# Ranks of a gate line by two comparisons a tile, from a line that each partition reads one element further on

## The chip, the cores and the metric

The kernel runs on one core of one Trainium2 chip. The metric is device time in microseconds (us) of one execution; several runs are made and the median is given. The engines of a core are TensorE (PE; PEld is its weight load), VectorE (DVE), ScalarE (ACT), GpSimd (POOL) and SyncE (SP), which issues most DMAs. Each engine works through its own instructions in program order and waits for others by semaphores.

## The reference

Attention with queries pooled in pairs, and behind it a mixture-of-depths layer: in each batch the 128 tokens with the highest gate scores go through a two-layer network, and the others pass unchanged.

```python
B, H, S, D = 8, 8, 1152, 64                       # attention
q_pool = q.reshape(B, H, S // 2, 2, D).mean(axis=3)
scores = q_pool @ k.T / sqrt(D)
attn = softmax(scores)                            # over the keys
x = (attn @ v), heads side by side                # (8, 576, 512)

scores = einsum('bsd,d->bs', x, w_gate)           # mixture of depths, F = 1024, capacity = 128
for b in range(B):
    top_idx = argpartition(-scores[b], capacity)[:capacity]
    xe = x[b, top_idx]
    ye = maximum(xe @ w1, 0) @ w2
    g = 1 / (1 + exp(-scores[b, top_idx]))
    out[b, top_idx] = x[b, top_idx] + g[:, None] * ye
```

## The kernel before

**Halves.** The work of the attention is cut into 8 batches x 4 pairs of heads x 2 halves of the 576 pooled queries: 64 halves, numbered from 0, eight to a batch. A method `run` writes out the order by hand; for half h it issues:

- at odd halves the loads of the pair after the next (`load_pair`: keys L744, queries L750, values L759) and the stores of an earlier pair (`stored`, L1023), all on SP;
- `scores`: 72 matmuls (L871) and nine exponentials on ScalarE (L878); they need the pair's `kT` and `qT`;
- `units("mid")`: pieces of the routing of earlier batches;
- `gated` (half h - 3) and `folded`: the sums of the exponentials. GpSimd adds two thirds of them in three instructions (`acc`, L910), VectorE sums the last third and then `acc` (`fold`, L915);
- at even halves `prepare_pair`: GpSimd pools the queries (L769), VectorE transposes keys into `kT` (L772) and queries into `qT` (L776);
- `weighted` (half h - 1): 72 matmuls with the values (L889); ScalarE copies the result (L897), GpSimd adds its two parts (L899), and `drained` transposes it on VectorE (L968);
- `normalized` and `divided` (L1012): the division by the sums, the latter on GpSimd;
- `units("end")`: more pieces of the routing.

**Routing.** `routed(b, part)` is a Python generator of one batch's routing. Each `yield` ends a piece; its value says where the next piece is issued: "mid", "sums" (between `folded` and `weighted`), or, for True, "end". One batch's pieces are thus spread over the halves of the next batch. The pieces are: the gate line of 576 scores is summed (L1067, L946) and written to HBM as a `row`; it is read back in two layouts, once whole into each partition (`sc_row`, L1083), and once token by token across partitions (`gate_sc`, L1084 and L1085: partition p has tokens p, 128 + p, and so on). The gate is max(score, -88) (L1099), an exponential (L1146), plus one (L1149) and a reciprocal. A token's rank is the number of tokens that come before it. For each of five tiles of 128 tokens (the last has 64), VectorE counts the tokens in earlier tiles with a score no lower (L1113), those from its own tile on with a higher score (L1122), and, by a triangular mask `before`, those of equal score earlier in its own tile (L1132, `tie`). Each count is two entries of the trace, the comparison and the read of its accumulator. Batches 0 to 5 cut this after tiles 1 and 3, batch 6 after tile 2, with `yield mid`, where `mid` is True for batches 6 and 7.

Ranks and gates go to HBM (L1162, `row_rank`) and come back in every partition (`lines`, L1166, 640 KB); two searches on VectorE (L1197) find the token and the gate of each slot; GpSimd gathers the tokens' rows by an indirect DMA (L1224); a copy through HBM and a transpose (L1237, L1254, L1262) turn them. In batch 7 the slots are found by a comparison `pick` (L1174) and matmuls with it (L1183) instead, with index and gate copied by ScalarE (L1190, L1191).

**The network.** Two batches are worked on together (`layers_of_two`, batches 0 and 1, and 2 and 3) by seven block products a layer (`seven_products`, L1358), with the weights' sums `tw` loaded in turn (L715). The result is added to the tokens' rows by `scaled` (L1451) and written back by an indirect DMA of GpSimd (`written`, L1300). Batches 4 and 5, and 6 and 7, are worked on in `ending`, where `first_layer` and `second_layer` (L1437, L1447) are generators too, and `pieces(unit, n)` issues n pieces of one. There `layer` is the first layer of batches 4 and 5, `third` that of 6 and 7, `second` a second layer, `old` what is left of batch 6's routing and `new` batch 7's. c11, c12, c21 and c22 are the quarters of a layer's result, s1 to s4 the sums that the next layer needs (`four_sums`, L1524). Values of the attention are stored (`stored`) before rows are gathered from the output.

Of the kernel before, what the change touches and what calls it, by code (L numbers as in the profile page):

```python
# [10 lines left out]
P = 128  # L11
BLK = 32

G = 3
F32 = mybir.dt.float32
# [6 lines left out]
def _rows_of(ap_1d: bass.AP, parts: int) -> bass.AP:  # L22

    return dataclasses.replace(ap_1d, ap=[[0, parts]] + [list(x) for x in ap_1d.ap])

# [509 lines left out]
class _Plain:  # L535
# [85 lines left out]
    def constants(self):  # L621
        nc, const = self.nc, self.const

        self.before = const.tile([P, P], F32, name="before")
        nc.gpsimd.memset(self.before[:, :], 1.0)
        nc.gpsimd.affine_select(
            out=self.before[:, :],
            in_=self.before[:, :],
            compare_op=ALU.is_gt,
            fill=0.0,  # L630
            base=0,
            pattern=[[-1, P]],
            channel_multiplier=1,
        )
# [39 lines left out]
    def weight_loads(self):  # L674
# [5 lines left out]
        for c in range(self.ND):  # L680
            yield self.nc.sync.dma_start(self.w1[:, c, :], w1[:, c, :])

# [326 lines left out]
    def divided(self, pair):  # L1009

        x = pair["x"] = self.work.tile([P, self.QB, BLK], F32, name="x")
        self.nc.gpsimd.tensor_tensor(  # L1012
# [44 lines left out]
    def routed(self, b, part):  # L1057
# [12 lines left out]
        sc = ffn.tile([P, NT], F32, name="gate_sc")  # L1070
# [6 lines left out]
        sc_row = ffn.tile([P, NT * P], F32, name="sc_row", bufs=1)  # L1077
        row = self.dram.tile([Sp], F32, name="row")
        nc.gpsimd.memset(sc[:, NF:], 0.0)
        nc.sync.dma_start(row.rearrange("(i n) -> i n", i=BLK), total[:, :])  # L1080

        def reads():
            nc.sync.dma_start(sc_row[:, 0:Sp], _rows_of(row[:], P))  # L1083
            nc.sync.dma_start(sc[:, 0:NF], row[0 : NF * P].rearrange("(t p) -> p t", p=P))  # L1084
            nc.sync.dma_start(  # L1085
                sc[0 : self.TAIL, NF:], row[NF * P :].rearrange("(t p) -> p t", p=self.TAIL)
            )
# [6 lines left out]
        if b < self.B - 2:  # L1094
# [5 lines left out]
            out=gate[:, :], in0=sc[:, :], scalar1=-88.0, scalar2=None, op0=ALU.max  # L1100
        )

        parts = ffn.tile([P, NT, 3], F32, name="rank_parts")
# [3 lines left out]
        rank = ffn.tile([P, NT], F32, name="rank")  # L1107
        for t, rows in tiles:
            at = t * P
            cmp = ffn.tile([P, Sp], F32, name="pick", bufs=1)  # L1110
            own = sc[0:rows, t : t + 1]
            if t > 0:
                nc.vector.tensor_scalar(  # L1113
                    out=cmp[0:rows, 0:at],
                    in0=sc_row[0:rows, 0:at],
                    scalar1=own,
                    scalar2=None,
                    op0=ALU.is_ge,
                    op1=ALU.add,
                    accum_out=parts[0:rows, t, 0:1],  # L1120
                )
            nc.vector.tensor_scalar(  # L1122
                out=cmp[0:rows, at:Sp],
                in0=sc_row[0:rows, at:Sp],
                scalar1=own,
                scalar2=None,
                op0=ALU.is_gt,
                op1=ALU.add,
                accum_out=parts[0:rows, t, 1:2],
            )  # L1130
            tie = ffn.tile([P, P], F32, name="pick", bufs=1)
            nc.vector.scalar_tensor_tensor(  # L1132
                out=tie[0:rows, 0:rows],
                in0=sc_row[0:rows, at : at + rows],
                scalar=own,
                in1=self.before[0:rows, 0:rows],
                op0=ALU.is_equal,
                op1=ALU.mult,
                accum_out=parts[0:rows, t, 2:3],
            )  # L1140
            cuts = (2,) if b == self.B - 2 else (1, 3)
            if t == cuts[0] < cuts[-1]:
                yield True
            if t == cuts[-1]:
                yield mid
# [687 lines left out]
```

## Time and profile before

| | |
|---|---|
| median of 3 runs | 689.88 us (689.51 to 690.7) |
| the profiled execution: time, span | 688.71 us, 686.9 us |
| mean granted TensorE clock | 0.994 of full speed |
| TensorE busy | 674.0 us (98%) |
| VectorE, GpSimd, ScalarE busy | 591.3 (86%), 501.1 (73%), 454.7 us (66%) |
| DMA, mean | 148 GB/s |

All times are from the start of the span, in us, durations in us unless marked ns. A line of the timeline has the start, the duration, engine, line of the kernel, operation, output <- input and shape, and in brackets the idle time of that engine before it, with what ended it. A line of groups ends with busy time in us, the mean of one in ns, and idle time before. A line of windows has the stretch, its length, busy time and count of PE, PEld, DVE, ACT and POOL, the granted TensorE clock, the mean number or share of the DMA queues at work, and GB/s. A value in the last columns is an average over the window.

Half h has its scores at about 7 us + 8.7 h, plus what the layers of batches 0 to 3 take in between; the scores of half 60 start at 585.14, those of half 63, the last, at 611.37, and `ending`'s first product stands at 624.57.

### The profile page before, as it was taken

How to read it: one execution, taken by the hardware profiler on the slowest of the kernel's cores; microseconds unless marked ns; L12 is line 12 of the kernel's file. 1: busy time of each engine (PE TensorE's matmuls, PEld its weight loads, DVE VectorE, ACT ScalarE, POOL GpSimd, SP SyncE). 2: the span in 40 equal slices, each digit the busy share in tenths (PEclk: the TensorE clock that was granted, in tenths of full speed). 3: DMA queues.
4: the chain of work that ended last, by engine and by line, in shares of the span. 5: the costliest groups of instructions: out<-in, count | busy, mean ns of one | idle time of the engine just before them, and what ended most of it. 6: DMA issues, size and time to landing. Idle time of an engine off the chain costs nothing.

```text
span 686.9 us, 23530 instructions
## 1 busy us (share of the span) xinstructions
PE 674.0 (98%) x9953; PEld 461.5 (67%) x9953; DVE 591.3 (86%) x880; ACT 454.7 (66%) x989; POOL 501.1 (73%) x485
## 2 busy tenths in 40 slices
PE   8999999999999999999999999999989999999996
PEld 6666666666666568676667768667657776668895
DVE  3878998999999986778899996696999999798864
ACT  5677777777777784837777776673767777873220
POOL 4788888879887883857798787393888879876011
PEclk9999999999999999999999999999999999999999
DMA  8888888858985885644988697571888848635210
GB/s 164 171 185 179 221 176 179 156 108 194 206 179 105 187 161 104 176 87 104 258 154 159 127 176 152 122 174 37 186 225 154 154 102 176 168 86 134 42 47 36
DMA packets 396642, 101.50 MB, mean 148 GB/s; under 512 B 376432, under 2 KB 380400, under 8 KB 395504
## 3 DMA queue, kind: packets, MB, share of 16 engines
q1 hardware_dynamic: 395008, 95.43, 67.0%
q0 software_dynamic: 1280, 4.20, 1.7%
q8 instruction: 79, 1.29, 0.8%
q10 hardware_dynamic: 240, 0.30, 0.2%
q14 instruction: 35, 0.29, 0.1%
HBM read 82.27 MB, written 17.62 MB: 145 GB/s over the span
## 4 chain that ended last, share of the span: by engine, by line
PE 81%; DVE 6%; DMA 5%; issue 3%; POOL 2%; ACT 1%; SPq 1%; ACTq 0%; POOLq 0%; DVEq 0%
PE ps L871 36%; PE ps L889 34%; PE ps L1358 7%; PE ps L1437 2%; PE ps L1447 2%; DMA kb<-in_k_dram 1%; POOL acc L910 1%; DVE fold L915 1%; DVE kT L772 1%; DMA lines<-row_rank 1%; DMA p<-in_q_dram 1%; DMA xe<-out_dram,index 1%; ACT p L878 1%; DMA gate_sc<-row 1%; DMA row<-total 0%
## 5 line engine op out<-in xcount | busy, mean ns | idle before, releaser
L878 ACT ACTIVATE p<-ps 128x576 f32<-128x576 f32 x576 | 321.4, 695 | 5.0 <-PE ps L871 4.3
L910 POOL TENSOR_TENSOR acc<-p 128x576 f32<-128x576 f32 x192 | 274.9, 1459 | 32.4 <-ACT p L878 32.1
L871 PE MATMUL ps<-qT,kT 64*64 64x288 f32 x4608 | 294.1, 405 | 3.6 <-DVE qT L776 2.9
L889 PE MATMUL ps<-p,v_sb 64*64 64x288 f32 x4608 | 291.5, 403 | 0.0
L871 PEld LDWEIGHTS ps<-qT,kT 64*64 64x64 f32 x4608 | 181.0, 133 | 104.4 <-ACT p L878 14.7
L889 PEld LDWEIGHTS ps<-p,v_sb 64*64 64x64 f32 x4608 | 178.6, 133 | 100.9 <-ACT p L878 13.5
L915 DVE TRANSPOSE_TENSOR_REDUCE fold<-p 128x54 f32<-128x1728 f32 x64 | 126.0, 1969 | 27.5 <-ACT p L878 27.0
L915 DVE TRANSPOSE_TENSOR_REDUCE fold<-acc 128x54 f32<-128x1728 f32 x64 | 124.3, 1943 | 10.2 <-POOL acc L910 10.0
L897 ACT COPY two<-ps 128x576 f32<-128x576 f32 x64 | 40.8, 638 | 132.7 <-PE ps L889 120.6
L899 POOL TENSOR_TENSOR av<-two 128x288 f32<-128x288 f32 x64 | 51.7, 809 | 70.6 <-ACT two L897 70.6
L772 DVE STREAM_TRANSPOSE kT<-kb 128x1152 f32<-128x1152 f32 x31 | 73.2, 2362 | 0.0
L978 POOL TENSOR_TENSOR prod<-avb,w_gate 128x288 f32<-128x288 f32 x64 | 51.8, 810 | 1.7 <-DVE red L1034 1.5
L769 POOL TENSOR_TENSOR qp<-qb 128x576 f32<-128x576 f32 x31 | 43.7, 1409 | 2.9 <-DMA qb<-in_q_dram 2.9
L968 DVE STREAM_TRANSPOSE avb<-av 128x288 f32<-128x288 f32 x64 | 28.5, 446 | 16.9 <-POOL av L899 16.9
L955 ACT ACTIVATE sums<-total,tiny 32x18 f32<-32x18 f32 x124 | 38.2, 308 | 5.6 <-DVE total L946 3.7
L1012 POOL TENSOR_TENSOR x<-avb,rec 128x576 f32<-128x576 f32 x32 | 37.0, 1156 | 0.0
L1132 DVE SCALAR_TENSOR_TENSOR pick<-sc_row,gate_sc,before 128x128 f32<-128x128 f32 (+1 forms) x40 | 30.7, 766 | 1.4
L940 ACT COPY groups<-sum 32x36 f32<-32x36 f32 x124 | 27.2, 219 | 4.4 <-DVE sum L925 2.8
L1034 DVE TENSOR_REDUCE red<-prod 128x9 f32<-128x288 f32 x64 | 27.8, 435 | 0.1
L925 DVE TENSOR_REDUCE sum<-fold 128x18 f32<-128x108 f32 x64 | 21.9, 342 | 2.2
L776 DVE STREAM_TRANSPOSE qT<-qp 128x576 f32<-128x576 f32 x31 | 23.2, 747 | 0.0
L1122 DVE TENSOR_SCALAR_CACHE_REDUCE pick<-sc_row,gate_sc 128x576 f32<-128x576 f32 (+4 forms) x40 | 21.6, 539 | 0.3
(170 smaller groups left out, 473.5 us busy)
## 6 DMA issues: line engine op xcount, KB each, us to landing
kb<-in_k_dram SPq DMA_DIRECT2D x124, 144.0 KB
qb<-in_q_dram SPq DMA_DIRECT2D x124, 144.0 KB
v_sb<-in_v_dram SPq DMA_DIRECT2D x31, 576.0 KB
out_dram<-x SPq DMA_DIRECT2D x128, 72.0 KB
tw<-tw SPq DMA_DIRECT2D x8, 1024.0 KB
lines<-row_rank SPq DMA_DIRECT2D x7, 640.0 KB
w<-in_moe_w_dram SPq DMA_DIRECT2D x8, 512.0 KB
tw<-tw SPq DMA_DIRECT2D x8, 512.0 KB
```

Source lines behind the costliest of these rows:

```text
L769: nc.gpsimd.tensor_tensor(out=qp[:, :, :], in0=pair["q"][:, :, 0, :], in1=pair["q"][:, :, 1, :], op=ALU.add)
L772: nc.vector.transpose(kT.rearrange("p (c i g) -> p c g i", c=self.NC, i=BLK), pair["k"].rearrange("p (g c) d -> p c g d", c=self.NC),)
L871: nc.tensor.matmul(sc[keys, j, 0:n], lhsT=pair["kT"][rows, c * P + keys.start : c * P + keys.stop], rhs=pair["qT"][rows, qs], start=True, ...
L878: nc.scalar.activation(p[:, c // G, c % G, :, :], sc[:, :, 0:n], AF.Exp, scale=self.scale)
L889: nc.tensor.matmul(av[j * self.D : (j + 1) * self.D, e, 0:n], lhsT=half["pair"]["v"][keys, j, c, :], rhs=half["p"][keys, c // G, c % G, j, :],
L897: nc.scalar.copy(two[:, :, :], av[:, :, 0:n])
L899: nc.gpsimd.tensor_tensor(out=half["av"][:, :], in0=two[:, 0, :], in1=two[:, 1, :], op=ALU.add)
L910: nc.gpsimd.tensor_tensor(out=acc[:, u, :], in0=units[:, 0, u, :], in1=units[:, 1, u, :], op=ALU.add)
L915: nc.vector.tensor_reduce(fold[:, a, :], of.rearrange("p u (m d) -> p (u m) d", d=BLK), AX.X, ALU.add, apply_transpose=True,)
L955: self.nc.scalar.activation(tot[rows, :], pair["total"][:, j * self.QB : (j + 1) * self.QB], AF.Identity, bias=self.tiny[0:BLK, 0:1],)
L978: self.nc.gpsimd.tensor_tensor(out=pair["prod"][:, ns, :], in0=pair["avb"][:, ns, :], in1=self.w_gate[:, hp : hp + 1, :].broadcast_to([P, ...
L1358: nc.tensor.matmul(args[0], lhsT=args[1], rhs=args[2], start=k == 0, stop=k == n - 1)
```

## The change

- The gate line is written to one of two lines in HBM (`gate_lines`) with 127 lowest numbers in front and behind. These pads are written once, after the loads of the weights (`gate_pads`: one memset on GpSimd, two DMAs on SP).
- One DMA reads it back: partition p gets 703 elements from element p on (`_next_of`). So element 127 + 128 t of partition p is the score of token 128 t + p, what lies before it are the tokens before, and the two other reads and the memset of `gate_sc` go.
- A tile's ranks are two comparisons: elements before its own with "no lower", those from its own on with "higher". The tie instruction, its mask `before` and a third of `rank_parts` go.
- Batch 6's cut after tile 2 is a "mid", so all of its later pieces come a step earlier (and `ending` issues one piece of `old` less). Batch 7 is no longer cut within the tiles; its exponential stands before them, as a piece of its own that is issued ahead of c12's piece of `layer`; its pick matmuls, index copies and gather are issued ahead of the last piece of `layer`, `four_sums` and the second piece of `third`.
- The last two pairs are divided on VectorE instead of GpSimd.
- In `layers_of_two` the quarters of the second layer's result lie in pairs side by side, and `scaled` adds 512 columns at once: two instructions instead of four.

```diff
+def _next_of(ap_1d: bass.AP, parts: int) -> bass.AP:
+    return dataclasses.replace(ap_1d, ap=[[1, parts]] + [list(x) for x in ap_1d.ap])
...
     def constants(self):
-        self.before = const.tile([P, P], F32, name="before")
-        nc.gpsimd.memset(self.before[:, :], 1.0)
-        nc.gpsimd.affine_select(
...
     def weight_loads(self):
...
+        self.gate_pads()
+        yield
+
+    def gate_pads(self):
+        n, edge = P - 1 + self.Sp, P - 1
+        lines = self.dram.tile([2, n + edge], F32, name="gate_lines", bufs=1)
+        self.gate_lines = [lines[i] for i in range(2)]
+        low = self.ffn.tile([P, self.NT + 1, P], F32, name="line", bufs=1)[0:2, 0, 0:edge]
+        self.nc.gpsimd.memset(low, -3.4028234e38)
+        for part in (lines[:, 0:edge], lines[:, n:]):
+            self.nc.sync.dma_start(part, low)
...
     def divided(self, pair):
-        self.nc.gpsimd.tensor_tensor(
+        ending = pair["b"] == self.B - 1 and pair["hp"] >= self.NPAIR - 2
+        engine = self.nc.vector if ending else self.nc.gpsimd
+        engine.tensor_tensor(
...
     def routed(self, b, part):
-        sc = ffn.tile([P, NT], F32, name="gate_sc")
...
-        sc_row = ffn.tile([P, NT * P], F32, name="sc_row", bufs=1)
-        row = self.dram.tile([Sp], F32, name="row")
-        nc.gpsimd.memset(sc[:, NF:], 0.0)
-        nc.sync.dma_start(row.rearrange("(i n) -> i n", i=BLK), total[:, :])
+        n = P - 1 + Sp
+        line = ffn.tile([P, NT + 1, P], F32, name="line", bufs=1)
+        near = line.rearrange("p t n -> p (t n)")
+        sc = line[:, 0:NT, P - 1]
+        row = self.gate_lines[b % 2]
+        nc.sync.dma_start(row[P - 1 : n].rearrange("(i n) -> i n", i=BLK), total[:, :])
 
         def reads():
-            nc.sync.dma_start(sc_row[:, 0:Sp], _rows_of(row[:], P))
-            nc.sync.dma_start(sc[:, 0:NF], row[0 : NF * P].rearrange("(t p) -> p t", p=P))
-            nc.sync.dma_start(
-                sc[0 : self.TAIL, NF:], row[NF * P :].rearrange("(t p) -> p t", p=self.TAIL)
-            )
+            nc.sync.dma_start(near[:, 0:n], _next_of(row[0:n], P))
...
+        if b == self.B - 1:
+            nc.scalar.activation(gate[:, :], gate[:, :], AF.Exp, scale=-1.0)
+            yield True
+        parts = ffn.tile([P, NT, 2], F32, name="rank_parts")
...
+        cuts = {self.B - 2: (2,), self.B - 1: (NT,)}.get(b, (1, 3))
         for t, rows in tiles:
+            own = t * P + P - 1
+            cmp = ffn.tile([P, NT, P], F32, name="pick", bufs=1).rearrange("p t n -> p (t n)")
+            for i, (part, op) in enumerate(((slice(0, own), ALU.is_ge), (slice(own, n), ALU.is_gt))):
                 nc.vector.tensor_scalar(
+                    out=cmp[0:rows, 0 : part.stop - part.start],
+                    in0=near[0:rows, part],
+                    scalar1=sc[0:rows, t : t + 1],
                     scalar2=None,
+                    op0=op,
                     op1=ALU.add,
+                    accum_out=parts[0:rows, t, i : i + 1],
                 )
-            tie = ffn.tile([P, P], F32, name="pick", bufs=1)
-            nc.vector.scalar_tensor_tensor(
...
             if t == cuts[-1]:
-                yield mid
+                yield "mid"
                 nc.scalar.activation(gate[:, :], gate[:, :], AF.Exp, scale=-1.0)
...
     def layers_of_two(self, tokens):
-        for i, of in enumerate(c):
-            token = tokens[i // 2]
-            if i % 2 == 0:
-                yield "mid"
-            to = token["xe"][0:w, i % 2 * half : (i % 2 + 1) * half]
-            self.scaled(to, of, token, to)
-            if i % 2:
-                yield True
-                self.written(token, token["index"])
+        for of, token in zip((third, room[:, 0, :]), tokens):
+            yield "mid"
+            self.scaled(token["xe"][0:w, :], of[0:w, 0 : self.Dm], token, token["xe"][0:w, :])
+            yield True
+            self.written(token, token["index"])
...
     def ending(self, halves, old):
-        pieces(old, 1)
         pieces(new, 1)
         pieces(layer, 2)
         for of in (halves[-3]["pair"], last):
             self.divided(of)
             self.stored(of)
         pieces(layer, 1)
         pieces(old)
-        pieces(layer, 3)
+        pieces(layer, 1)
+        pieces(new, 1)
+        pieces(layer, 2)
...
-        pieces(new, 3)
+        pieces(new, 2)
         pieces(layer)
         self.four_sums(c, s)
         pieces(third, 1)
-        pieces(new, 1)
```

## The prediction

> **What bounds the kernel now.** I read the page first, then the waits of TensorE, the windows of the two places where it idles, and the timeline there.
>
> ```profile
> PE 674.0 (98%) x9953; PEld 461.5 (67%) x9953; DVE 591.3 (86%) x880; ACT 454.7 (66%) x989; POOL 501.1 (73%) x485
> ```
>
> TensorE is busy 98% of the span, and the change alters none of its matmuls. So VectorE time that is saved counts only where TensorE waits for VectorE. The waits (line, whom for: us, times, longest) say where:
>
> ```profile
> PE ps L871 <- DVE qT L776: 2.9, 2, 2.5
> ...
> PE ps L1183 <- DVE pick L1174: 0.9, 1, 0.9
> PE ps L1447 <- DVE s L1524: 0.6, 1, 0.6
> ```
>
> All of it is at three places: before the scores at 345.39 (0.40 us) and at 513.39 (2.51), and in the ending at 647.73 and 649.62 (0.89, 0.56). The windows (length, busy us of each engine, PEclk) show a second cost:
>
> ```profile
> 511.00:514.40 3.40, 1.01 (x17) 0.80 (x21) 3.40 (x5) 2.28 (x9) 3.40 (x4) 1.00 0.83 158
> 514.40:518.00 3.60, 3.60 (x36) 2.48 (x32) 3.57 (x4) 2.85 (x5) 2.10 (x4) 0.53 0.95 153
> ```
> ```profile
> 647.60:651.00 3.40, 2.71 (x16) 2.51 (x17) 2.67 (x5) 0.63 (x1) 0.00 (x0) 1.00 0.02 5
> 651.00:654.40 3.40, 3.40 (x9) 2.68 (x8) 1.91 (x4) 1.01 (x4) 1.03 (x1) 0.50 0.00 0
> ```
>
> After a window with little matmul work TensorE runs the next 3.4 us at half clock. In the first, 72 score matmuls took 6.28 us where their neighbours take 4.54: 1.74 lost. In the second, 24 matmuls of L1447 took 7.14 where the 24 from 637.92 took 5.35: 1.79 lost. The whole prize is therefore 2.51 + 1.74 + 0.40 + 0.89 + 0.56 + 1.79 = 7.9 us, with 0.28 more at 626.90.
>
> Why is VectorE late at 513? It runs in order, without a gap, from 477.61 (batch 4's routing):
>
> ```profile
> 500.38 5.13 DVE L1197 SCALAR_TENSOR_TENSOR pick<-lines,token 128x640 f32<-128x640 f32 x1
> 500.67 4.14 POOL L910 TENSOR_TENSOR acc<-p 128x576 f32<-128x576 f32 x3
> ```
> ```profile
> 334.30 1.05 POOL L1300 DMA_INDIRECT out_dram<-xe,index  x1 [2.62 <-DVE sum L925]
> ...
> 334.47 0.79 DVE L1197 SCALAR_TENSOR_TENSOR pick<-lines,token 128x640 f32<-128x640 f32 x1
> ...
> 335.38 1.42 POOL L910 TENSOR_TENSOR acc<-p 128x576 f32<-128x576 f32 x1
> ```
>
> The same search is in both. In batch 2 it gets in ahead of GpSimd's sums (L910) and takes 0.79; in batch 4 GpSimd starts 0.29 us after it, and it ends only 0.69 after the third sum: 5.13. That is 4.3 us, and the transposes (kT, qT) queue behind it.
>
> **The change part by part.** The profiled run took 688.71 us, 1.84 more than its span; the median of the runs is 689.88, so 1.17 is carried on top.
>
> *Ranks.* The tie instructions go:
>
> ```profile
> L1132 DVE SCALAR_TENSOR_TENSOR pick<-sc_row,gate_sc,before 128x128 f32<-128x128 f32 x32 | 21.1, 659 | 1.1
> ...
> L1132 DVE SCALAR_TENSOR_TENSOR pick<-sc_row,gate_sc,before 64x64 f32<-64x64 f32 x8 | 9.6, 1194 | 0.3
> ```
>
> That is 30.7 us, and 3.1 for their 40 accumulator reads. Each tile's two comparisons now cover 703 elements instead of 576: by the rows of 128 (345 ns) and 576 elements (812 ns) one element is 1.04 ns, so 0.13 a tile, and tile 0 has one instruction more (0.28): 0.8 a batch, 6.4 in all. VectorE loses 27 us; nearly all of it lies beside a busy TensorE and is worth nothing.
>
> *Read of the line.* One DMA of 128 rows of 2812 bytes replaces 128 of 2304 and 576 of 4 bytes; SP issues one (0.35 us) instead of three (0.35 + 0.43 + 0.51). I take 3.5 us from issue to landing, as batch 6's reads took in the chain of waits (3.48): fewer pieces, 22% more bytes. Bounds: 2.7 (the last scatters, chain) to 4.94 (the 5120-byte rows of `lines`, chain). Batches 0 to 5 have over 6 us of cover; batch 7 is below. *Scaling.* Two instructions of 512 instead of four of 256, twice: a pair of 256 takes 0.80 undisturbed (328.67), one of 512 by 1.04 ns an element 0.67; caught by GpSimd (1.45 and 1.62 at 480.65 and 482.02) one catch instead of two. *Pads, constants.* A memset and two small SP stores at half 10, by SP's issue of keys at 501.04 (0.61) some 1.2 us ahead of keys issued at 99.23 and transposed at 120.52: nothing, and 1.2 us of SP without that cover. The two GpSimd instructions of `before` (0.48 us at 1.45) kept nobody waiting: nothing.
>
> *Batches 2 and 4.* After 477.61 tile 4 costs 1.1 (639 and 64 elements) instead of 2.3 us, the first scaling ends near 481.0 instead of 483.65, then VectorE waits for ScalarE's exponentials (481.60) and for L910 (about 483.7). So the first search (before: 491.59, done 494.46 because L910 held it) starts near 489.4, where L910 would start near 489.25: almost a tie. If it gets in, or at the first boundary as the ties did at 480.44, all behind it is 3 to 4 us earlier. If not, 0.3, and the second search has another 0.13 from the scaling, against the 0.29 by which it lost. Bounds: 0 to 4.65 us (2.51 + 1.74 + 0.40); a loss is rival 4. I take the upper end: two races, either suffices, and in batch 2 the second is already won.
>
> The trace's rows settle two questions on which the skill would say otherwise. The Trainium skill (SBUF — State Buffer, section "SBUF: two separate sides") states that the shared port is held for one instruction; by that the search would have lost one L910 (1.4 us), not the 4.3 seen, and of the 4.65 only the 0.40 were to be had. The Trainium skill (TensorE: Matmul & The Clock Gate, section "HAM oscillation — how this bites in real kernels") gives as the rule no idle gaps above about 3.4 us; by it neither gap would cost clock, and the gain would be 4.2 us.
>
> *Batch 6, its second cut from "end" to "mid" of half 61.* Everything it issues moves: tiles 3 and 4, row_rank and lines on SP (from 612.89 to about 606.9, past nothing but finished stores), both searches one step earlier, gather and copy too. Cost: GpSimd's gate + 1 now stands before the three L910 of half 61 and waits for the exponential, which on ScalarE stands behind the spread that ends at 601.0. L910 starts near 601.5 instead of 599.25. Cover: VectorE wants that sum at 607 (L910 done 605.7). The search waits for `lines` until about 613.3 (1.5 us idle). GpSimd's last sums end near 623.6, VectorE's last fold 0.8 earlier than 626.39. No TensorE work hangs on it before 626.90, whose 0.28 may go.
>
> *Ending.* The two divisions go from GpSimd (2 x 1.15) to VectorE: 0.75 each (512 elements take 0.69), in front of the layer's sums; the 0.8 above and 0.6 of idle there pay for it. The read is issued near 632.6 and lands near 636.1; gate max stands at about 636.8. If it landed later, sum c12 behind it would be late; TensorE wants c12 at 639.65, ready about 638.1. Ranks then run 637.7 to 643.3 (5.6 instead of 6.67), and this idle goes:
>
> ```profile
> 645.57 0.21 ACT L1146 ACTIVATE gate<-gate 128x5 f32<-128x5 f32 x1
> 645.81 0.17 DVE L1149 TENSOR_SCALAR gate<-gate 128x5 f32<-128x5 f32 x1 [1.46 <-ACT gate L1146]
> ...
> 646.29 1.29 DVE L1174 TENSOR_TENSOR pick<-token_line,rank 128x640 f32<-128x640 f32 x1
> ...
> 647.73 1.33 PE L1183 MATMUL ps<-meta,pick 128*128 128x2 f32 x10 [0.89 <-DVE pick L1174]
> ```
>
> Pick is done near 645.1. On TensorE the pick matmuls now stand before 16 matmuls of the third layer, free at 645.0: wait 0.1 to 0.4. Behind them on ScalarE the index copies (646.8) stand before relu c21 (647.4), then sum s1 (648.1); TensorE wants it at 648.35. So L1447 starts near 648.3 instead of 649.62: 1.3 us (bounds 0.5 to 1.45). The gather leaves near 647 instead of 653.13, so the transposes at 656.72 do not hold the rest back. Poor matmul time in a row falls from 2.78 us (0.89 + 1.33 + 0.56) to some 1.6, so I take the half clock to go too: 1.79, or 0 if not.
>
> **Sum:** 4.65 + 1.3 + 1.79 = 7.7 us; 688.71 - 7.7 = 681.0 for a profiled run, 682.2 on the median.
>
> **The rivals.**
> 1. The ending keeps its half clock, as 1.33 us of nearly empty pick matmuls remain: 689.88 - 5.95 = 683.9. Chance 0.25; the likeliest case has 0.42.
> 2. Batch 4's search is caught again: 0.4 + 0.3 and the ending's 1.3 to 3.1 are left: 686.1 to 687.9. For it: 0.15 and 0.2 us decide both races. Chance 0.15.
> 3. No change: the waits only change their names (lines, near, relu), within 0.2%, which is about what a measurement can tell: 689.9. Chance 0.05.
> 4. Slower: the race of batch 2 turns. Place: the search at 334.47, which leads L910 by 0.91 us; it decides once that lead falls under 0.3. Price as in batch 4: 2.11 more stall and 1.74 of clock, 3.85; batch 4 unchanged and 1.3 from the ending: 689.88 + 3.85 - 1.3 = 692.4. For it: VectorE's new timing is only estimated. Against: the lead comes from the gather's landing, which moves along with the search. Chance 0.13.
>
> **How the numbers follow.** Faster by over 0.2%: 0.42 + 0.25 + 0.15 = 0.82; within: 0.05; slower: 0.13. The range ends at 688.2, rival 2's worse end with 0.3 of the runs' spread, and leaves out rivals 3 and 4 (0.18). Below, all idle and the whole clock (8.2) give 681.7, less 0.8 for the runs' spread 680.9.
>
> **What would show it.** Right: no tie instructions, 10 comparisons a batch at some 5.6 us, no TensorE gap at 513, no search above 1.6 us in batch 4, clock 1.00 after the pick, pick waiting under 0.5. Wrong: a search of 3 us or more with a gap before L871; VectorE waiting for the line's DMA ahead of gate max; half clock in a place that had none.

## The result, and the profile after

The changed kernel takes **684.44 us** (median of 7 runs, 683.28 to 685.26), the kernel before beside it 689.38 (687.15 to 690.70): ratio 0.9933, 95% interval 0.9915 to 0.9951. The prediction was 682.2 with a range of 680.9 to 688.2. The profiled execution took 683.79 us, its span is 682.0, against 688.71 and 686.9 before.

The busy line of the page, and waits of TensorE on the other engines (line, whom for: us, times, longest):

```profile
PE 671.3 (98%) x9953; PEld 456.7 (67%) x9953; DVE 566.1 (83%) x814; ACT 454.0 (67%) x989; POOL 499.6 (73%) x474
```
```profile
PE ps L877 <- DVE qT L782: 1.1, 2, 0.6
...
PE ps L1171 <- DVE pick L1162: 0.3, 1, 0.3
PE ps L877 <- ACT two L903: 0.2, 1, 0.2
```

VectorE has 25.2 us less to do; TensorE waits for kT and qT for 1.1 us instead of 2.9, for the pick 0.3 instead of 0.9, and no longer for s. A new name is there: the scores of half 63 wait for ScalarE's copy `two`. The windows of the two old places:

```profile
511.00:514.40 3.40, 2.84 (x52) 1.72 (x48) 3.40 (x5) 2.32 (x8) 3.40 (x4) 1.00 0.79 124
514.40:518.00 3.60, 3.60 (x65) 2.58 (x61) 3.56 (x4) 3.60 (x8) 3.60 (x4) 1.00 0.96 178
643.60:647.00 3.40, 3.34 (x27) 3.34 (x28) 1.67 (x3) 1.10 (x4) 1.03 (x1) 1.00 0.02 5
647.00:650.40 3.40, 3.40 (x17) 2.99 (x17) 2.85 (x6) 0.89 (x2) 0.00 (x0) 1.00 0.26 77
```

The granted clock is 1.00 in all four. Batch 4's two searches in the timeline:

```profile
490.89 4.45 DVE L1185 SCALAR_TENSOR_TENSOR pick<-lines,token,token_line 128x640 f32<-128x640 f32 x1
```
```profile
501.12 0.78 DVE L1185 SCALAR_TENSOR_TENSOR pick<-lines,token 128x640 f32<-128x640 f32 x1
501.12 1.71 POOL L1288 DMA_INDIRECT out_dram<-xe,index  x1 [2.41 <-DVE sum L931]
...
502.86 1.43 POOL L916 TENSOR_TENSOR acc<-p 128x576 f32<-128x576 f32 x1
```

The first search is held longer than before (4.45 us, 2.87 before), the second takes 0.78 instead of 5.13, since GpSimd's sums (L916, formerly L910) start 1.73 us after it instead of 0.30.

**Where the 4.9 us of span went**, from the starts of the same matmuls in both traces:

| place | predicted | measured |
|---|---|---|
| batch 2's wait, 345 | -0.40 | +0.17 (0.57 is left) |
| batch 4's wait, 513 | -2.51 | -1.95 (0.56 is left) |
| half clock behind it | -1.74 | -1.69 |
| half 63's scores | 0 | +0.72 (5.26 instead of 4.54) |
| ending, from half 63's end | -3.09 | -3.6 |
| first queries, before half 0 | 0 | +0.37 |
| scores of halves 18, 26, 42, 58 | 0 | +1.08 |

### The profile page after: what moved, and what is told of

It is laid out like the page before. It is cut to its first block, busy times and chain, and to the rows that moved or that the text cites. A ratio compares the mean times of both kernels' runs of the same rounds, so it can differ in the third digit from the quotient of the medians.

```text
span 682.0 us, 23423 instructions
## 1 busy us (share of the span) xinstructions
PE 671.3 (98%) x9953; PEld 456.7 (67%) x9953; DVE 566.1 (83%) x814; ACT 454.0 (67%) x989; POOL 499.6 (73%) x474
## 4 chain that ended last, share of the span: by engine, by line
PE 79%; DVE 6%; POOL 5%; issue 4%; DMA 3%; ACT 1%; ACTq 0%; POOLq 0%; DVEq 0%
PE ps L877 35%; PE ps L895 35%; PE ps L1346 7%; POOL acc L916 3%; DVE pick L1121 2%; DMA xe<-out_dram,index 1%; PE ps L1421 1%; ACT p L884 1%; DVE kT L778 1%; PE ps L1431 1%; POOL qp L775 1%; DMA p<-in_q_dram 1%; DVE fold L921 1%; POOL out_dram L1288 1%; POOL prod L984 0%
## 5 line engine op out<-in xcount | busy, mean ns | idle before, releaser
L916 POOL TENSOR_TENSOR acc<-p 128x576 f32<-128x576 f32 x192 | 275.8, 1465 | 35.1 <-ACT p L884 34.7
L877 PEld LDWEIGHTS ps<-qT,kT 64*64 64x64 f32 x4608 | 178.1, 132 | 105.7 <-ACT p L884 18.8
L905 POOL TENSOR_TENSOR av<-two 128x288 f32<-128x288 f32 x64 | 51.2, 800 | 70.7 <-ACT two L903 70.5
L1121 DVE TENSOR_SCALAR_CACHE_REDUCE pick<-line 128x127 f32<-128x127 f32 (+4 forms) x80 | 45.3, 566 | 2.4
L1020 POOL TENSOR_TENSOR x<-avb,rec 128x576 f32<-128x576 f32 x30 | 34.8, 1160 | 0.0
L1288 POOL DMA_INDIRECT out_dram<-xe,index x7 | 8.4, 1198 | 20.8 <-DVE xe L1435 10.3
```

What stands on the lines that cost most here:

```text
L877: nc.tensor.matmul(sc[keys, j, 0:n], lhsT=pair["kT"][rows, c * P + keys.start : c * P + keys.stop], rhs=pair["qT"][rows, qs], start=True, ...
L905: nc.gpsimd.tensor_tensor(out=half["av"][:, :], in0=two[:, 0, :], in1=two[:, 1, :], op=ALU.add)
L916: nc.gpsimd.tensor_tensor(out=acc[:, u, :], in0=units[:, 0, u, :], in1=units[:, 1, u, :], op=ALU.add)
L1121: nc.vector.tensor_scalar(out=cmp[0:rows, 0 : part.stop - part.start], in0=near[0:rows, part], scalar1=sc[0:rows, t : t + 1], scalar2=None ...
```

## The experiments

Each set of runs has its own runs of the kernel before, and these vary: a median of 689.68 us in the first set (684.72 to 692.94), 688.47 in the second (684.92 to 694.45), 686.96 in the third (684.52 to 691.49). So kernels are compared within a set first. The changed kernel was not run again in these sets; beside it a kernel stands by its ratio to the kernel before, and there differences under some 0.003 (2 us) lie within the intervals. One run of each kernel is profiled, and it need not be a typical one.

**First set: the change cut in parts.**

*The main loop's part alone* (`e1`): batch 6's and batch 7's cuts, the order of the pieces and the two divisions as before (part of the edit is shown):

```diff
-        if b == self.B - 1:
-            nc.scalar.activation(gate[:, :], gate[:, :], AF.Exp, scale=-1.0)
-            yield True
-        cuts = {self.B - 2: (2,), self.B - 1: (NT,)}.get(b, (1, 3))
+        cuts = (2,) if b == self.B - 2 else (1, 3)
...
-                yield "mid"
+                yield mid
```


> The changed kernel without its parts for the ending: batch 7 is cut within its tiles again, its exponential and picks stand where they stood, the last two pairs are divided on GpSimd, batch 6's second cut is an 'end' again. Ranks by two comparisons, the shifted read and the merged scaling stay. My theory (the main loop's gain is batch 4's search and the half clock behind it, nothing else): the wait at 513 stays at about 0.56 us and no half clock follows (2.51 + 1.74 before), the wait at 345 stays near 0.57, half 63 takes 4.54 us again instead of 5.26. In the ending the ranks are one us shorter than before, so the pick's wait of 0.89 falls to 0 to 0.2, but the 0.56 behind it and the half clock (1.79) may stay. Together 685.3 to 687.0 us, a ratio of 0.994 to 0.9965. If instead the ending's parts bring the whole gain, this kernel stands at 688.5 to 690 and the wait at 513 may be back. If the slower loads of the start and the small delays of the halves (1.4 us together in the changed kernel) come with the shifted read, they are seen here as well; if they come with batch 6's move or the ending, they are gone.

685.46 us (684.48 to 688.76), ratio 0.9958 (0.9930 to 0.9986). The wait at 513 is 0.28 us with no half clock, half 63 takes 4.55. But the pick waits 0.89 as before, though the ranks are 0.5 us shorter (6.18 instead of 6.67): VectorE idles 2.37 us there for batch 7's exponential, which stands on ScalarE behind a copy that ends at 642.75. The ending's half clock is gone in this profile, but its time is not gained: the gather of batch 7 leaves at 650.22 (645.46 in the changed kernel), and the transposes behind it wait:

```profile
PE ps L1255 <- DMA lines<-out_dram,index: 1.7, 1, 1.7
```

From the end of half 63's scores on, the span takes 70.5 us here, 71.0 before and 67.3 after. Shorter ranks alone are worth next to nothing in the ending.

*The ending's part alone* (`e2`): the kernel before with the new order, batch 7's cut and the divisions; batch 6's cut stays.

> The kernel before with the ending's parts alone: the last two pairs divided on VectorE, batch 7's exponential ahead of its tiles and no cut within them, its picks, copies and gather issued earlier. Ties, the three reads and the four scalings stay, and batch 6 keeps its cut. My theory: the stall of batch 4 stays as it was (2.51 us and 1.74 of half clock), half 63 takes 4.54 us. In the ending the ranks still take 6.67 us, 1.1 more than in the changed kernel, so the pick waits 1.0 to 1.5 us instead of 0.32 and the half clock behind it (1.79) is a toss-up: a gain of 0.3 to 2.5 us, 687 to 689 us, ratio 0.996 to 1.0. If the order in the ending is enough by itself, no half clock and 3 us gained: 686.3 us, ratio 0.9955. If the ending's order is worth nothing without the shorter ranks: 689.4, ratio 1.0.

687.90 us (685.17 to 693.9), ratio 0.9987 (0.9955 to 1.0019), so unclear. The pick waits 1.33, with half clock behind it. The surprise is in the loop, which is that of the kernel before:

```profile
334.28 5.47 DVE L1202 SCALAR_TENSOR_TENSOR pick<-lines,token 128x640 f32<-128x640 f32 x1
...
334.92 4.13 POOL L910 TENSOR_TENSOR acc<-p 128x576 f32<-128x576 f32 x3
```

Here batch 2's second search is caught (TensorE waits 2.81 at 347.60) and batch 4's is not. The same code loses the race now in one batch, now in the other; that may be a good part of the spread of the kernel before, but only these two profiles show it. And a lead of 0.64 us over L910 is not enough.

*Batch 6's cut back at "end"* (`e3`):

```diff
-                yield "mid"
+                yield mid
...
+        pieces(old, 1)
```


> The changed kernel with one edit undone: batch 6's second cut is an 'end' again, and the ending issues one piece more of it. My theory: moving it cost half 63 0.71 us, since GpSimd's gate and VectorE's tiles 3 and 4 stand ahead of the sum that ScalarE's groups wait for at 609.8; without the move half 63's 72 score matmuls take 4.54 us again instead of 5.26, and the gap of 0.28 to 0.45 us before the third layer's sums at 626.9 comes back. Net 0.3 to 0.7 us faster than the changed kernel: 683.7 to 684.1 us. The rival, that the move pays in the ending because batch 6's gather and transposes come earlier: up to 1 us slower than the changed kernel, 684.5 to 685.5 us. The prediction's own value was no effect in the loop and 0.28 at 626.9.

683.20 us (682.07 to 686.07), ratio 0.9918 (0.9889 to 0.9947). Half 63 takes 4.55 us, and the gap at 626.9 does not come back. The pick's matmuls wait 0.72 us, for ScalarE's copy of `p`, and a half-clock stretch follows, so that the ending of this profile takes 69.4 us instead of 67.3; `e8` below, with the same cut back, has no such stretch and takes 67.5. So the move costs 0.7 us in half 63; what it brings in the ending is open, 0.2 us by `e8` and 2.0 by this profile. By the ratios (0.9918 and 0.9933) the two kernels cannot be told apart.

*The first search earlier* (`e7`):

```diff
-                yield True
+                yield "sums" if b in (2, 4) else True
```


> The changed kernel with the first search of batches 2 and 4 issued between the sums and the weighted values, that is ahead of the transposes of keys and queries of that half instead of behind them. My theory: what is left of the two waits (0.57 us at 345 and 0.56 at 513) hangs on the first search, which GpSimd's sums hold for 4.4 us in both batches; placed where GpSimd is past its three sums, it takes 0.8 us and both waits go: 1.1 us faster than the changed kernel, 683.3 us. Rival: there it stands behind the sum that needs GpSimd's acc, and pushes kT and qT of its own half by 0.8 us, so that one wait is exchanged for another: 684.4 us or up to 1 us more. Second rival: the search does not get in there either, since GpSimd is at its next work (the parts' sums); 4 us again, and a stall of 2 to 3 us with half clock: 687 to 689.

682.68 us (682.13 to 684.86), ratio 0.9907 (0.9879 to 0.9936). The time fits the theory, the trace does not: the search takes 1.43 us there, and in the profiled run, the slowest of the ten (it has a half-clock stretch in half 0 that costs 1.5 us), the waits are 0.55 and 0.93. They are not the search's doing. VectorE then idles 3.67 us at 508.19 for GpSimd's sum: what is late is GpSimd, whose three sums stand behind the write L1288, and that behind the gather. Where this kernel gains is open.

**Second set: VectorE work put back.** A spare two-input instruction a tile, like the old tie, its result not used; the batches differ:

```diff
+            if b in (0, 1, 3, 5):
+                nc.vector.scalar_tensor_tensor(out=tie[0:rows, 0:rows],
+                    in0=near[0:rows, own : own + rows], scalar=sc[0:rows, t : t + 1],
+                    in1=self.ones[0:rows, 0:rows], op0=ALU.is_equal, op1=ALU.mult,
+                    accum_out=spare[0:rows, :])
```

*Batches 0, 1, 3 and 5* (`e5`):

> The changed kernel with the tie instruction put back as spare work (its result is not used) in batches 0, 1, 3 and 5, where no wait of TensorE hung on VectorE before. VectorE gets back 20 instructions, some 15 us with their accumulator reads. My theory, that VectorE's relief is worth nothing there: 684.4 us, within 0.5 of the changed kernel, and no new wait of TensorE. If the time follows VectorE's load (25 us less work gave 4.9 us), it would be 3 us slower: 687.4.

684.30 us (682.9 to 685.4), ratio 0.9943 (0.9921 to 0.9964): the median is as expected, but the trace has a wait that neither theory named. The scores of half 63 wait 2.35 us for `two`, with a half-clock stretch behind:

```profile
PE ps L877 <- ACT two L903: 2.4, 1, 2.4
```

The profiled run, the slowest of the seven, thus has a loss of 4.35 us in half 63 behind a loop that was 2 us ahead: its wait at 513 is gone (lead 0.97) and halves 18, 26, 42 and 58 take 4.54 to 4.57 us each. Whether the faster runs have that loss too is not known.

*Batches 2 and 4* (`e6`):

> The changed kernel with the same spare tie instructions in batches 2 and 4 alone: 10 instructions, 7 to 8 us of VectorE. The shifted read and the merged scaling stay. My theory, that the ties decide when the searches of batches 2 and 4 meet GpSimd's sums: one of the two searches, in some runs both, is held past a second meeting and TensorE waits 2.5 to 2.8 us with half clock behind it in some runs; 2 to 4 us slower than the changed kernel, 686.4 to 688.5 us, with a wide spread of the runs like that of the kernel before. Rival, that the merged scaling or the shifted read brought the gain of the loop: 684.4 us and waits of 0.6 at both places as without the ties.

682.81 us (681.78 to 685.59), ratio 0.9932 (0.9906 to 0.9957). My theory falls: the ties do not decide the races. Both second searches win, with leads of 1.75 and 0.82, and the wait at 513 is gone. The traces show why the ties cannot reach the second race: in every profile that has the first search in its old place, it ends 0.69 us after GpSimd's third sum, whether it starts 0.4 us after the first of the three (after), 1.2 (here) or 2.0 (before). What is saved ahead of it is lost in it.

*Batch 7* (`e9`):

> The changed kernel with the spare tie instructions in batch 7 alone, 5 instructions. My theory: the ranks take 1.1 us longer more (6.67 before), so the pick waits about 1.3 us on TensorE instead of 0.32, as in the kernel before with the ending's parts alone; whether a half-clock stretch follows depends on how the idle time falls into the 3.41 us steps in which the granted clock is shown. 1.0 us slower without it, 2.7 with it: 685.4 to 687.1 us. Rival, that the ending's order alone brings its gain and the ranks of batch 7 do not matter: 684.4.

686.84 us (685.31 to 690.42), ratio 0.9989 (0.9964 to 1.0013), so no gain over the kernel before is left that is clear of noise. The pick waits 2.39 us. But the ranks take 8.08 us here, more than the 6.67 before, so the spare ties cost more than the old ones did, and `e2` is the better measure. `before`, `e1`, `e2` and `after` make a square of the waits of TensorE: neither edit 0.89 + 0.56 us, shorter ranks alone the same and 1.68 for the late gather, the new order alone 1.33 with half clock behind it, both 0.32. The ending's gain needs both.

*The merged scaling alone* (`e4`), on the kernel before:

```diff
-        for i, of in enumerate(c):
...
-            self.scaled(to, of, token, to)
+        for of, token in zip((third, room[:, 0, :]), tokens):
+            yield "mid"
+            self.scaled(token["xe"][0:w, :], of[0:w, 0 : self.Dm], token, token["xe"][0:w, :])
```


> The kernel before with the merged scaling alone (two instructions of 512 elements instead of four of 256, twice). The prediction gave it 0.13 us ahead of the search that it said was lost by 0.29. If that is right, the search of batch 4 still loses in most runs: 689 us, ratio 0.998 to 1.0, the same spread as before. If merging is what turns the search, since one instruction less is caught by GpSimd's sums (1.45 and 1.62 us for pairs of 256): the wait at 513 is gone in most runs, 685.5 to 686.5 us, ratio 0.995.

685.71 us (684.27 to 687.02), ratio 0.9963 (0.9949 to 0.9977). An edit that I gave 0.13 us turns the loop, with all ties in place:

```profile
502.11 1.05 POOL L1300 DMA_INDIRECT out_dram<-xe,index  x1 [2.28 <-ACT p L878]
502.24 0.77 DVE L1197 SCALAR_TENSOR_TENSOR pick<-lines,token 128x640 f32<-128x640 f32 x1
...
503.20 2.78 POOL L910 TENSOR_TENSOR acc<-p 128x576 f32<-128x576 f32 x2
```

The traces together show how. All times count from the end of the index of the first search (L1209 or L1197), which releases GpSimd's gather; lead is how long the second search starts before GpSimd's sums:

| kernel, batch | gather takes | write starts, takes | search starts | lead | search takes |
|---|---|---|---|---|---|
| before, 4 | 1.06 | +4.93, 1.05 | +5.72 | 0.30 | 5.13 |
| `e2`, 2 | 1.06 | +5.27, 1.06 | +5.72 | 0.64 | 5.47 |
| before, 2 | 1.06 | +5.54, 1.05 | +5.72 | 0.91 | 0.79 |
| `e2`, 4 | 1.06 | +5.76, 1.68 | +5.72 | 1.74 | 0.78 |
| `e6`, 4 | 1.32 | +5.34, 1.05 | +5.60 | 0.82 | 0.78 |
| `e4`, 4 | 1.32 | +5.47, 1.05 | +5.59 | 0.96 | 0.77 |
| after, 4 | 1.32 | +5.59, 1.71 | +5.59 | 1.73 | 0.78 |

The search takes 0.78 us and keeps that length if it is done when the sums start; a lead of 0.64 loses, one of 0.82 wins. The other profiles with the searches in their old place agree: with two scalings all 18 second searches win, with leads from 0.82 to 2.11; with four (`e12` below included) four of six do. The sums stand behind the write, and the write waits for the gather to land: in the profile before it lands 3.8 us after its issue in batch 4 and 4.5 in batch 2, in `e2` 4.7 and 4.2, in `e4` 4.4 and 5.4. So the race is a fixed chain on VectorE against a transfer that varies. One instruction of 512 elements where two of 256 stood brings the search 0.13 earlier and makes GpSimd's gather beside it 0.26 longer: 0.39 more lead for the same transfer. By an estimate from these rows, five of the 18 would have led by only 0.43 to 0.58 us without it.

Between a search and a DMA issue of GpSimd it matters which starts first. Where the write starts ahead of a search that wins, by 0.03 to 0.26 us, it takes 1.05 us. Where it starts with the search or inside it, it ends 0.93 to 0.95 us after the search's end in 13 cases of 13; so it takes 1.05 to 1.71 us, and the sums start 1.73 to 1.77 after the search. The gather behaves alike: it ends 0.93 us after the scaling instruction within which it starts. In batch 4 a write that was made longer saves the search and leaves a wait of 0.28 to 0.99 us at 513 (after, `e1`, `e2`, `e3`, `e9`); where it took 1.05 and the search won (`e4`, `e5`, `e6`, `e10`, `e11`, `e12`), that wait is gone.

**Third set: the race, the ranks, batch 6.**

*The change without the merged scaling* (`e12`), the edit of `e4` undone:

> The changed kernel with the merged scaling alone undone: four instructions of 256 elements again in the layers of batches 0 to 3. The runs so far put the loop's gain on a race: the second search of batches 2 and 4 (0.78 us) keeps its length where it starts at least 0.8 us before GpSimd's three sums and takes over 5 us where it leads by 0.3 or 0.64. Both count from the same instruction, the index of the gather: the search comes 5.72 us after it with four scalings and 5.59 with two; GpSimd's gather instruction takes 1.06 with four and 1.32 with two, so the lead is 0.39 longer with two. Theory now: with four scalings and everything else of the change the lead is short again in part of the runs; median 685.5 to 689 with a spread of 4 us or more, and in the profile either a search over 5 us at one of the two places and a wait of 2 us or more, or a lead over 0.8. The first theory (the shorter ranks turn the races): 684.4 us, spread 2 us, as the changed kernel.

682.88 us (680.32 to 684.08), ratio 0.9936 (0.9911 to 0.9961). My expectation fails: both races are won, with leads of 1.06 and 0.87 (the gather lands 4.6 and 4.4 us after its issue), and the spread stays under 4 us. The profiled run is the fastest of the eight. So merging is enough by itself (`e4`), and these runs show no need of it beside the rest. Counted from the end of its issue the gather lands 3.6 and 3.4 us later here, 2.8 to 3.6 in the kernel before and in `e2`: no sign that another part of the change makes it land later. Chance is the simpler reading, but with six searches it is not shown.

*All but the ranks and the read* (`e11`): the kernel before with the edits of `e2` and `e4`.

> The kernel before with the merged scaling and the ending's parts, but with the ranks as before (ties, three reads, batch 6's cut at 'end'): all of the change except what its first words name. If the ranks and the shifted read are worth nothing outside the ending: the merged scaling's 685.7 us less the ending's gain without shorter ranks (the pick waits 1.3 us there, the half clock comes in part of the runs): 684 to 685.5 us, so the same as the changed kernel or up to 1 us slower. If the shorter ranks carry the ending, as the spare ties in batch 7 say (2.4 us slower with them): 685.5 to 687 us.

684.29 us (682.48 to 688.43), ratio 0.9957 (0.9933 to 0.9981). Beside `e12`, of the same set, that is 1.4 us more; beside the changed kernel (0.9933) the intervals overlap. Its profile has the loss in the ending: 0.96 us of waiting before the sums at 622.76 and 1.68 for the pick, with a half-clock stretch behind it (643.93 to 647.34). In the loop there is only a wait of 0.93 at 345.

*Spare ties in batches 0, 1, 3 and 5, batch 6's cut back* (`e10`): the edits of `e5` and `e3`.

> The changed kernel with the spare ties of batches 0, 1, 3 and 5 (results not used) and with batch 6's cut back at 'end'. With the spare ties and batch 6's cut moved, TensorE was 2.0 us ahead of the changed kernel at half 62 and lost 4.35 in half 63, where the copy behind VectorE's sum of 609.95 held the scores for 2.35 us. Theory: that loss is batch 6's tiles standing ahead of that sum; with the cut back, half 63 takes 4.54 us and what the loop has gained stays: 680.5 to 682 us, faster than the changed kernel although VectorE has 15 us more to do. Rival: the loss is GpSimd's own lateness at half 60 (VectorE waited 4.15 us for its sum there instead of 1.78), which the spare ties of batch 5 cause: half 63 still waits over 1.5 us, 683.5 to 684.5 us.

685.22 us (683.15 to 687.5), ratio 0.9966 (0.9947 to 0.9986). Half 63 takes 4.74 us, which speaks for batch 6's tiles, though TensorE was also 1.6 us later there than in `e5`, by a half-clock stretch at the start. But the time that the theory gave is missed: VectorE is still late, and TensorE waits 1.34 us at 625.89 and 0.80 for the pick instead. The rival's lateness is real too. GpSimd's timeline shows where it begins, here and in `e8`, which has no spare ties:

```profile
587.63 0.73 POOL L1324 TENSOR_TENSOR s<-xeT 128x256 f32<-128x256 f32 x1 [3.15 <-DVE xeT L1262]
```
```profile
582.95 0.73 POOL L1312 TENSOR_TENSOR s<-xeT 128x256 f32<-128x256 f32 x1 [0.78 <-DVE xeT L1250]
```

With spare ties, GpSimd waits 3.15 us for VectorE's transposed rows of batch 5 (0.78 without); its `acc` of half 60 is late, and VectorE loses 4.16 us waiting for it at 594.67 (1.80 without). So VectorE's relief in batch 5 is worth something after all: it reaches GpSimd and comes back. Beside `e12`, of the same set, this kernel is 2.3 us slower.

*The first search earlier and batch 6's cut back* (`e8`): the edits of `e7` and `e3`.

> The changed kernel with the first search of batches 2 and 4 issued between the sums and the weighted values, and with batch 6's cut back at 'end'. Each alone stood at 682.7 and 683.2 us. If the two add up: half 63 takes 4.54 us (0.7 less), the gap before the third layer's sums comes back at most 0.3: 682.0 us, and a narrow spread as with the first search moved. If what the moved search gains was gained at half 63 or in the ending: 682.7 to 683.2, as each alone.

**680.55 us** (679.86 to 681.56), ratio 0.9900 (0.9873 to 0.9928), the fastest of all. The 682.0 expected came from medians of the first set, whose kernel before was 2.7 us slower than this set's, so the two gains do not do more than add up; beside `e12`, of the same set, it is 2.3 us faster. Its interval overlaps those of `e3`, `e7` and the changed kernel. The waits at 345 and 510 are 0.23 and 0.25, half 63 takes 4.55:

```profile
PE ps L1171 <- DVE pick L1162: 0.5, 1, 0.5
PE ps L877 <- DVE qT L782: 0.5, 2, 0.2
```

## Why the prediction was right, and where not

The sum was 7.7 us for a profiled run and 4.9 came. The places and signs of the main terms hold; the point and the cause of the race, the cover of batch 6's move, the length of the ranks and the claim that other relief of VectorE is worthless do not. That the median lies in the range owes something to luck: the race was won through the merged scaling, which the sum had at 0.13 us, and losses that it did not foresee took 2.2 us.

**Batches 2 and 4 (4.65 predicted, 3.47 measured).** The second of the two races was won, as the value taken assumed, and with batch 4's 5.13 us of search the half clock went. Three parts were wrong. The point from which a race decides is not a lead of 0.3 but about 0.8, the search's own length: "lost by 0.29" was about 0.5. The lead does not come from VectorE's shorter ranks (`e6`), since the first search swallows what they save; the merged scaling alone brings it (`e4`), by the search's 0.13 us and the gather's 0.26, a row that I did not look at. And the 0.40 and what is left of 2.51 hang on GpSimd's sums behind the write, so a won race does not remove them: 0.57 and 0.56 stay. The first race was lost outright (L916 starts 0.38 us ahead); that cost nothing more.

The Trainium skill (SBUF — State Buffer, section "SBUF: two separate sides") warns that GpSimd cannot write the descriptors of its own DMAs while VectorE runs an operation in a two-port performance mode. The rows show the same in kind beside two-input instructions, which the warning does not name: the gather's 1.06 and 1.32, the write's 1.05 and 1.71. The section also states that whichever engine starts first has the shared port for its whole instruction. By that the search, which led by 0.30 us in batch 4, would have lost nothing; the 1.4 us that the prediction took from this section do not follow from it. The search and the write keep to that rule, the search and the sums do not: 5.47 us in `e2`, with a lead of 0.64 and an end 0.69 us after the third sum.

**Batch 6's move (0 predicted, 0.72 lost).** I had put the whole cover in VectorE's wish for GpSimd's sum at 607, and asked who waits for the tiles, not what stands behind them. They stand ahead of the sum of half 62; ScalarE's spread of it waits, and behind that in ScalarE's order `two` and the exponentials:

```profile
609.78 0.91 ACT L946 COPY groups<-sum 32x36 f32<-32x36 f32 x4 [3.27 <-DVE sum L931]
...
610.60 0.62 ACT L903 COPY two<-ps 128x576 f32<-128x576 f32 x1
611.13 1.16 ACT L884 ACTIVATE p<-ps 128x576 f32<-128x576 f32 x2
```

`e3` shows it: 4.55 with the cut back. The other profiles agree: half 63 takes 5.25 to 8.89 us in the six that have the move and 4.54 to 4.74 in the eight that do not. That no TensorE work hangs on it before 626.90 was the sentence that failed.

**Ending (3.09 predicted, 3.6 measured).** Order and most prices fit, and the 0.28 us at 626.90, which the sum left out, went as well. The ranks take 6.2 us instead of the 5.6 foreseen, since each comparison now starts 0.04 us after the accumulator read before it instead of beside it; a division on VectorE takes 0.74 (0.75); the pick's wait is 0.32 (0.1 to 0.4); the gap before the second layer is gone. The pick's wait is 1.0 us shorter than in `e2` because the ranks are 0.5 shorter and VectorE comes to them 0.5 earlier, counted back from the pick's place on TensorE. The shifted read, taken at 3.5 us, landed 3.1 to 3.3 us after its issue for batch 7 in the three profiles that show that landing (`e6`, `e10`, `e12`). The gather's early leaving, a side remark of the prediction, is a condition of the gain: in `e1` it left late, and the 1.79 us of clock were not gained. That only the two edits together bring the gain was not said.

**The half clock as a term** was right in the profile and weaker than it looked. The length of an idle stretch does not decide it. In `e9` the stretch with the pick's wait of 2.39 has 1.02 us of matmuls and full clock follows; in `e3` one with a wait of 0.72 has 2.69 us and half clock follows:

```profile
643.58:646.99 3.41, 1.02 (x10) 0.85 (x9) 3.14 (x11) 0.58 (x1) 0.00 (x0) 1.00 0.00 0
646.99:650.40 3.41, 3.41 (x26) 3.30 (x27) 1.81 (x3) 0.75 (x3) 1.03 (x1) 1.00 0.13 20
```
```profile
641.96:645.37 3.41, 2.69 (x23) 2.50 (x22) 1.79 (x2) 1.28 (x4) 0.27 (x1) 1.00 0.02 5
645.37:648.79 3.42, 3.42 (x16) 3.15 (x15) 3.30 (x6) 0.07 (x2) 0.77 (x1) 0.50 0.26 77
```

What decides stays open. In four profiles (`e4`, `e7`, `e9`, `e10`) such a stretch stands in half 0 as well, which takes 7.9 to 8.1 us there and 6.5 in the others; these 1.5 us belong to none of the edits. The Trainium skill (TensorE: Matmul & The Clock Gate, section "HAM oscillation — how this bites in real kernels") asks for no idle gap above about 3.4 us; here 0.72 was enough in one run and 2.39 was not in another.

**"Nearly all worthless".** Spare ties in batches 2 and 4 cost nothing (`e6`), so there the claim holds. In batch 7 they cost some 2 us (`e9`), which the ending's step implied. In batches 0, 1, 3 and 5 they make VectorE and GpSimd late at half 60, which the prediction missed; the price is 4.35 us in half 63 of `e5`'s profile, though not in its median, and in `e10` the two waits of 1.34 and 0.80. The relief itself was also over-counted: the prediction's own terms give 0.93 us a batch for the longer comparisons (5 x 0.13 + 0.28), not 0.8, and VectorE lost 25.2 us of work, not 27.

**Not of the change.** The 1.08 us of halves 18, 26, 42 and 58 are a matter of the run: their four excesses over 4.54 sum to 0.6 in the profile before and 1.7 after, but to about nothing in `e5`, `e8`, `e10`, `e11` and `e12`, which have the same matmuls and mostly the same reads. In some runs halves 34 and 50 show it too (4.7 to 4.8 us). All four kernels of the third set, which ran on another chip than the first two sets, are without it in these four halves; whether the chip or chance decides is not shown, and the cause was not found. The 0.37 us ahead of half 0 belongs to the first loads and also varies: `e12`, which has the change's loads, starts 0.30 earlier than before.

**Rivals.** The measured 684.4 lies nearest to rival 1's 683.9, but not for its reason: the profile after has no half clock in the ending. Rival 4's mechanism, batch 2's race turned, is real; it happened in `e2`, at a lead of 0.64.

## What to carry to other kernels

When a stall is a race between two engines that hold each other up, find the common event from which both are counted and table their offsets over several runs. The instruction that moves the lead may be a short DMA issue on the other engine, and a race that is decided by tenths belongs in the range, not in a sum. A piece that is moved in a hand-written order delays everything behind it on its engine, so follow those consumers, not only the piece's own. Work taken off an engine with slack can still pay where it hands data to a third engine; and one profiled run can show a gain and a loss that its median does not, so read both.

## What the runs showed of the hardware that was not expected

- A two-input VectorE instruction that starts inside GpSimd's run of sums ends 0.69 us after the last of them, even one started 0.64 us ahead of the first (5.47 us instead of 0.78).
- GpSimd's indirect DMA issue does not hold the search (0.77 to 0.83 us beside it). It takes 1.05 us if it starts first; if it starts with the search or inside it, it ends 0.93 to 0.95 us after the search's end in 13 cases of 13 and takes up to 1.71 us.
- A half-clock stretch of 3.41 us followed a wait of 0.72 us in one run, and none followed 2.39 us in another.
- The same matmuls with the same producers cost 0 to 1.8 us more in all in four halves, depending on the run.
